# Talking-heads attention, Fourier mixing and an FFN: loads, statistics and the last transposes at the seam of two stages moved

## The chip, the cores and the metric

One core of a Trainium2 chip runs the kernel. The metric is device microseconds (us) of one execution, and less is better. Each engine has its own instruction stream and takes it in order: PE (TensorE, matmuls; its weight loads are shown as PEld), DVE (VectorE), ACT (ScalarE), POOL (GpSimd) and SP (SyncE, which here only issues DMAs). PE writes to PSUM; ACT and DVE evacuate from there to SBUF.

## What is computed

Two blocks follow each other, for 8 batches of 448 rows, 12 heads of 64, 768 columns, all in float32:

```python
scores = scale * q @ k^T                              # per batch and head
scores = einsum('bhij,hg->bgij', scores, w_pre)       # mix the heads
attn = exp(scores - max); attn = attn / (sum(attn) + 1e-9)
attn = einsum('bhij,hg->bgij', attn, w_post)          # mix them again
x = (attn @ v), heads side by side                    # 448 x 768 a batch
u = x + real(fft(fft(x, axis=1), axis=2))
un = (u - mean(u)) / sqrt(var(u) + 1e-6)
out = u + relu(un @ w_ch1) @ w_ch2                    # w_ch1 768 x 3072
```

## The kernel before

**Two stages.** `mix_phase` makes u of all batches and writes it to DRAM (`u_scr`, and `u_rev` for the mirrored rows). `ffn_phase` reads u back in 7 tiles of 512 rows and does the FFN. Both are matmul work on PE; a float32 matmul of the program is two records in the trace.

**Mixing.** A batch is 23 steps, all batches 184 steps, run by the loop at lines 932 to 964. In step s PE makes the pre-mix matmuls of step s+2 (L616, tile `mx`) and the post-mix matmuls of step s (L650, tile `po`), 16 records each. Between the two, DVE takes the maximum (L623), ACT the exponential (L630) and POOL the scaling by the row sum (L640). The mixing needs heads and rows side by side on partitions, so SP gathers each step's scores from tile `Sb` to tile `Kr` with four DMAs (L605), four steps ahead. The order of the operations within a step is written out by hand (`ORDERS`, two alternating lists).

**What fills the steps.** Other work is put between by due times. `due(kind, at, fn)` queues `fn` for step `at`; the kinds are `QK` (scores, L588, evacuated by ACT at L451), `AV` (attention times V, L680), `full` (transposes and Fourier matmuls) and `none` (loads and what needs no PSUM). `none` entries are issued at the start of a step (line 934). `full` and the PE kinds return evacuations that are queued in `pend` and issued at the next `flush`. Let f be the first step of the last batch (161): line 894 sets it. Around it:

- `emit_x` (L724): the transpose of the attention's result `XT` to `X`, four groups a batch, due at f+13, f+23, f+28 and f+29 (`AT_X`). A memset (L713) and a spill of the last AV group complete `XT` before the last two.
- `fold` (line 732, L745 to L766): sums and differences on POOL that the Fourier matmuls need, queued in `folds` and taken two a step until step f+19, later by `fold_rest`.
- `emit_z` (L789) and `emit_s2` (L805 on PE, L816 and L818 on DVE): the two Fourier stages. Those of a batch fall 39 to 49 steps after its start, so those of batch 6 run in the last batch's steps, and those of batch 7 in the FFN. After the last `emit_s2` of a pair, `store` writes u: plain DMAs on SP (L837), scattered ones on POOL (L828), and for the second pair a single row afterwards (L834), which two nested entries of the list `later` put two steps behind.
- V loads (L543) of the batch's own V at f+3 to f+7, on POOL; the loads of q and k for the next batch, which the last batch does not have; the conversion and storing of weights (`wts.deal`, L225 loads and L233 stores on POOL).

**The lead.** `_Lead` (line 319) prepares FFN tile 0 within the last mixing batch, so that the FFN can begin at once: `load` (L365) fetches its rows on POOL's queue, twelve DMAs, two a step; `stats` makes mean and variance on DVE (L370, L371); `power` makes the scale and shift on POOL (L375 to L378); `norm` applies them on ACT (L382); `turn` transposes on PE (L394) and evacuates half on ACT, half on DVE (L397); `total` makes differences of sub-blocks on DVE (L408). The rows' buffers are those of raw q and k, a ring of four.

**The FFN.** Both products use 7 products of sub-blocks in place of 8 (`ORDER`), with six chunks of the 3072 middle columns, two of them (`c` 0 and 1) of the kind the change touches. `first` multiplies a tile by a chunk of w_ch1: seven products of 12 records (L1169). `second` multiplies the result by w_ch2 (L1245), eight records for each product. In chunk 0 the same loop also prepares the next tile: its rows come in by `load_u` (L1064, SP), its statistics stand in `first` (L1085, L1086), its `power` after the last of them (L375 again), its `norm` (L1096) and `turn` (L1105, evacuated at L1107) in `second`. `store_ub` (L1119) writes a tile's sub-blocks to DRAM, for the next chunk.

**What sets the order.** Within `tc.manual_schedule(engines=...)` the named engines follow the program's order; the others are ordered by a planner with costs of its own. In mixing PE, DVE, ACT and POOL are named, in the FFN (chunks 0 and 1) PE and DVE. SP is never named, and DMAs that POOL issues can stand elsewhere than in the program's order too.

**The seam.** `mix_phase` returns after step f+29. What is left in `fill["full"]` (the z and s2 of batch 7) becomes `parts`, which `next_part` issues between FFN products: in tile 0's `second` after products 3 to 6, in tile 1's `first` after products 0 and 3 to 6. `ffn_phase` starts with line 1393:

```python
    with tc.manual_schedule(engines={ET.PE, ET.DVE, ET.Pool}):
        lead.total(3, pub)
        fold_rest()
```

Of the kernel before, what the change touches and what calls it, by code (L numbers as in the profile page):

```python
# [17 lines left out]
B, NH, S, D = 8, 12, 448, 64  # L18
# [394 lines left out]
def mix_phase(ctx, tc, rest, ident, q, k, v, w_pre, w_post, u_scr, u_rev, wts, lead):  # L413
# [6 lines left out]
    nc = tc.nc  # L420
# [27 lines left out]
    pend, folds, later = [], [], []  # L448
# [396 lines left out]
    def due(kind, at, fn):  # L845
        fill[kind].append((at, len(fill[kind]), fn))
# [4 lines left out]
    for b in range(B):  # L851
        f = b * GS
        at_t = [(a, nm, xx) for xx, at in enumerate(AT_T) for nm, a in zip("qk", at)]
        if b == 0:

            for i, xx in enumerate(START):
                for j, nm in enumerate("kq"):
                    for y in range(2):
                        due("none", -40, lambda xx=xx, nm=nm, y=y: emit_load_qk(0, xx, nm, y))
                    due("full", 2 * i + j - 20, lambda xx=xx, nm=nm: emit_xpose(0, xx, nm))  # L860
                for n in range(2):
                    due("QK", 2 * i + 2 + n - 20, lambda n=n, xx=xx: (emit_qk(n, xx), n))
            for pr in range(3):
                for y in range(2):
                    due("none", -40, lambda pr=pr, y=y: emit_load_v(0, pr, y))
        else:
            for at, (a, nm, xx) in zip(AT_L, sorted(at_t, key=lambda e: e[0])):
                for y in range(2):
                    due("none", f + at[y] - GS,
                        lambda b=b, xx=xx, nm=nm, y=y: emit_load_qk(b, xx, nm, y))  # L870
            for xx, at in enumerate(AT_T):
                for nm, a in zip("qk", at):
                    due("full", f + a - GS,
                        lambda b=b, xx=xx, nm=nm: emit_xpose(b, xx, nm))
        for pr in range(3 if b else 0):
            for y in range(2):
                due("none", f + AT_V[pr][y], lambda b=b, pr=pr, y=y: emit_load_v(b, pr, y))
        for n in range(0 if b else 2, NBL):
            for xx in range(3):
                due("QK", f + BLOCK_AT[n] - 7 + AT_QK[n][xx],  # L880
                    lambda n=NBL * b + n, xx=xx: (emit_qk(n, xx), n))
        for n in range(NG):
            for pr in range(3):
                due("AV", f + GROUP_AT[n + 1] + AT_AV[n][pr],
                    lambda a=b * NG + n, pr=pr: (emit_av(a, pr), None))
            at, gi = AT_X[n]
            due("full", f + at, lambda g=groups[b * NG + gi]: emit_x(g))
        for n, at in enumerate(AT_Z):
            due("full", f + at, lambda b=b, n=n: emit_z(b, n // 2, n % 2))
        for pair in range(2):  # L890
            for par in range(2):
                due("full", f + AT_S[pair][par],
                    lambda b=b, pair=pair, par=par: emit_s2(b, pair, par))
    f = (B - 1) * GS
    due("none", f, lambda: nc.gpsimd.memset(lead.mhalf[:, :], -0.5))
    for x in range(TB // P):
        for y in range(2):
            due("none", f + 1 + 2 * x + y, lambda x=x, y=y: lead.load(x, y))
        due("none", f + 8 + x, lambda x=x: lead.stats(x))
        due("none", f + (14, 15, 19, 20)[x], lambda x=x: lead.norm(x))  # L900
        due("full", f + 18 + 2 * x, lambda x=x: lead.turn(x, ms_tile))
    due("none", f + 12, lambda: lead.power(lead.mv))
    for n in range(3):
        due("none", f + 26 + n, lambda n=n: lead.total(n))
    due("none", 0, lambda: wts.deal(0))
    due("none", -39, emit_load_mix)
    due("none", -3, emit_mix)
# [23 lines left out]
    with tc.manual_schedule(engines={ET.PE, ET.DVE, ET.Activation, ET.Pool}):  # L931
        while s <= TOT - GS + AT_X[-1][0]:
            old = len(later)
            n = take("none", s)
# [35 lines left out]
            folds.pop(0)()  # L970

    def part(fn, tile_fn):
        while later:
            later.pop(0)()
        ms.append(tile_fn)
        if fn:
            for e in fn():
                e()
# [14 lines left out]
ORDER = (0, 4, 5, 1, 6, 2, 3)  # L993
# [11 lines left out]
def ffn_phase(ctx, tc, rest, ident, u_scr, u_rev, wts, ub_scr, out, fold_rest,  # L1005
# [4 lines left out]
    nc = tc.nc  # L1010
# [5 lines left out]
    pub = pool("pub", 3)  # L1016
# [29 lines left out]
    def next_part():  # L1046
        if parts:
            parts.pop(0)(lambda: ppx.tile([P, 512], F32, name="ms", tag="ms"))

    us, ubs, w1, w2, wt = {}, {}, {}, {}, {}  # L1050
# [59 lines left out]
    def total(t, n):  # L1110
        o, a, b = TOTALS[n]
        nc.vector.tensor_tensor(ubs[t, o][:, :, :], ubs[t, a][:, :, :],
                                ubs[t, b][:, :, :], op=ALU.subtract)
        if n == 3:
            store_ub(t)

    def store_ub(t):
        for i in ORDER:
            nc.sync.dma_start(out=ub_scr[t][i], in_=ubs[t, i][:, :, :])  # L1119

    H11, H22, H21, HS1, HS2, H12, H12S = range(7)
    LHS = (H11, H12, H12S, H22, HS1, HS2, H21)
# [21 lines left out]
    def first(n, st, beside):  # L1144

        c, t = divmod(n, NTB)
# [10 lines left out]
        for k, i in enumerate(ORDER):  # L1157
            if deep and t == 0:
                halves(ORDER2[k], (nc.vector, nc.gpsimd)[k % 2])
            if i in OPENS and ACC[i] not in ps:  # L1160
                ps[ACC[i]] = ps_tile(ACC[i])
            p = ps[ACC[i]].rearrange("p (m t) -> p m t", m=FM)
            ub = ubs.pop((n, i))
            for m in range(FM):
                for kc in range(NK):
                    for fn in beside.pop(done, ()):
                        fn()
                    done += 1
                    mm = nc.tensor.matmul(p[:, m, :], w1[i][:, kc, m * P:(m + 1) * P],  # L1169
                                          ub[:, kc, :],  # L1170
                                          start=i in (0, 4, 1)[:3 - seed] and m == kc == 0,
                                          stop=kc == NK - 1, skip_group_check=True)
                    if n == k == m == kc == 0:
                        tc.keep_in_program_order(mm)
            if i == 0 and seed:
                ps["Q"] = ps_tile("Q")
                nc.scalar.copy(out=ps["Q"][:, :], in_=ps["P"][:, :])
            elif i == 0:
                nc.scalar.copy(out=h11, in_=p)
            elif i == 4:  # L1180
                nc.scalar.copy(out=h22, in_=p)
            elif i == 5:
                nc.scalar.copy(out=h21, in_=p)
            elif i == 1 and seed:
                nc.scalar.activation(h11, p, ACTF.Relu)
            elif i == 1:
                vec.tensor_tensor(h11, h11, p, op=ALU.add)
                nc.scalar.activation(h11, h11, ACTF.Relu)
            elif i == 6:
                vec.tensor_tensor(h22, h22, p, op=ALU.add)  # L1190
                nc.scalar.activation(h22, h22, ACTF.Relu)  # L1191
                if deep:
                    quarters(nc.gpsimd, hq, h, H11, H22 + 1)
            elif i == 2:
                vec.tensor_tensor(h21, h21, p, op=ALU.add)
                nc.scalar.activation(h21, h21, ACTF.Relu)
            else:
                nc.scalar.activation(h12, p, ACTF.Relu)
            x = k - 3 * (n == 0)
            if norms and 0 <= x < NT2:  # L1200
                stats(t + 1, x)
                if x == NT2 - 1:
                    power(t + 1)
            if n == 1 and k not in (1, 2):
                next_part()
            if deep:
                wts.deal(DEALS[t > 0][k])
            elif i != 2:
                wts.deal(2 if norms else 3 if c == 0 else 4)
            if i == 2:  # L1210
                vec.tensor_tensor(hs1, h21, h22, op=ALU.add)
                vec.tensor_tensor(hs2, hs1, h11, op=ALU.subtract)
                if deep:
                    quarters(vec, hq, h, HS2, HS2 + 1)
                vec.tensor_tensor(h21, h11, h21, op=ALU.subtract)
            if t == NTB - 1 and c + 1 < NC:
                load_w1(c + 1, i)
            if NTB <= n + 1 < NC * NTB:
                new_ub(n + 1, i)
                nc.sync.dma_start(out=ubs[n + 1, i][:, :, :],  # L1220
                                  in_=ub_scr[(n + 1) % NTB][i])
# [168 lines left out]
    us[0] = lead.u  # L1390
    ET = mybir.EngineType
    with tc.manual_schedule(engines={ET.PE, ET.DVE, ET.Pool}):
        lead.total(3, pub)
        fold_rest()
    for i in ORDER:
        ubs[0, i] = lead.ub[i]
    with tc.manual_schedule(engines={ET.PE, ET.DVE}):
        for i in ORDER:
            load_w2(0, i)
        store_ub(0)  # L1400
        parts_ = [(c, k) for c in range(1, NC) for k in range(NK + FM)]
        for n in range(DEEP * NTB):
            c, t = divmod(n, NTB)
# [6 lines left out]
                load_u(n + 2)  # L1410
            st = {}
            first(n, st, {})
            second(n, st)
            if c == 0:
                wts.deal(1000)
# [98 lines left out]
```

## Time and profile before

| What | Value |
|---|---|
| median of 3 runs | 2360.4 us (2359.66 to 2360.79) |
| the profiled execution's own time | 2356.83 us |
| its span, first to last instruction | 2355.1 us |
| mean granted TensorE clock | 0.992 |
| steps of the last batch, f to f+22 | 718.2 to 810.6 us |
| last attention matmul (L680) starts | 823.15 us |
| first FFN product (L1169) starts | 830.72 us |
| mean rate of DMAs | 181 GB/s |

Times within the profile count from the span's start. A line such as `L650` is a line of the kernel. In a row of the timeline stand start, length, engine, line, operation, result tile <- input tiles, form and number of instructions; a bracket tells how long the engine stood idle before it and what ended that. In a row of waits stand the waiting engine, tile and line, what it waited for, the total, how often, and the longest. Busy shares are averages over stages with different limits; the two stages and their seam are therefore read apart.

### The profile page before, as it was taken

Reading aid. Unit: us, or ns where it says so; the run is one execution under the profiler, and the core shown is the slowest. Engines: PE = TensorE matmul, PEld = TensorE weight load, DVE = VectorE, ACT = ScalarE, POOL = GpSimd, SP = SyncE. Lnnn points to the kernel's source line nnn. Section 1 sums busy time; section 2 is a strip of 40 time slices with the busy share of each in tenths; the row PEclk is TensorE's granted clock in tenths of the full one; section 3 lists DMA queues with packets and bytes.
Section 4 is the critical chain, followed back from the end, with each engine's and each line's share of the span. In section 5 each row is a group of like instructions: output and inputs, shape, how many; then the busy total and the mean of one; then the engine's idle time right before and its main releaser. Section 6 shows DMA issues by size and latency. Waiting matters only on the chain.

```text
span 2355.1 us, 59472 instructions
## 1 busy us (share of the span) xinstructions
PE 2286.6 (97%) x22600; PEld 1717.5 (73%) x22600; DVE 1673.8 (71%) x3596; ACT 1103.0 (47%) x3085; POOL 1138.8 (48%) x1692
## 2 busy tenths in 40 slices
PE   6999999999999989999999999999999999999998
PEld 3455555554554667777777779998999999999998
DVE  3768777887777647785676766678776777776556
ACT  4766766676676522322222234443444344444434
POOL 3577977878777532121343443335333533443333
PEclk9999999999999999999999999999999999999999
DMA  7565655656646555567787876549546945684553
GB/s 161 160 174 175 178 177 155 199 171 181 188 150 189 193 180 195 178 223 269 225 208 230 241 240 181 144 138 271 149 132 169 258 125 166 175 229 107 148 129 67
DMA packets 213481, 425.60 MB, mean 181 GB/s; under 512 B 39080, under 2 KB 135744, under 8 KB 213198
## 3 DMA queue, kind: packets, MB, share of 16 engines
q1 hardware_dynamic: 141758, 278.78, 34.7%
q0 software_dynamic: 65440, 141.05, 27.4%
q8 instruction: 181, 2.97, 0.5%
q10 hardware_dynamic: 6000, 1.97, 0.4%
q14 instruction: 102, 0.84, 0.1%
HBM read 213.16 MB, written 129.39 MB: 145 GB/s over the span
## 4 chain that ended last, share of the span: by engine, by line
PE 57%; DVE 3%; issue 2%; DMA 1%; POOL 1%; ACT 0%; SPq 0%; POOLq 0%; DVEq 0%
PE psP L1169 17%; PE psP L1302 10%; PE psR L1169 9%; PE psR L1302 5%; PE psP L1245 5%; PE psQ L1169 4%; PE psR L1245 3%; PE psQ L1302 3%; PE psQ L1245 1%; PE psQ L1105 1%; DVE hq L1133 1%; DMA w<-wst 0%; DMA u<-u 0%; DMA w2t<-w 0%; POOL w L233 0%
## 5 line engine op out<-in xcount | busy, mean ns | idle before, releaser
L640 POOL TENSOR_SCALAR PP<-PP,rcp 128x448 f32<-128x448 f32 x368 | 234.8, 647 | 207.0 <-DVE rcp L638 165.0
L630 ACT ACTIVATE PP<-mx,nmx 128x448 f32<-128x448 f32 x368 | 230.2, 630 | 188.0 <-DVE nmx L623 174.3
L623 DVE TENSOR_REDUCE nmx<-mx 128x1 f32<-128x448 f32 x368 | 213.7, 618 | 137.3 <-PE mx L616 133.7
L1336 POOL DMA_DIRECT2D out_dram<-od x109 | 133.1, 1406 | 283.0 <-DVE od L1333 159.9
L1133 POOL TENSOR_TENSOR hq<-h 128x256 f32<-128x256 f32 (+1 forms) x168 | 104.3, 621 | 291.8 <-ACT h L1191 171.5
L616 PE MATMUL mx<-Kr,kw 60*32 60x448 f32 x2944 | 211.2, 551 | 15.6 <-DMA Kr<-Sb 14.1
L1333 DVE TENSOR_TENSOR od<-od 128x768 f32<-128x768 f32 x196 | 188.9, 975 | 52.5 <-ACT od L1330 50.6
L588 PE MATMUL ms<-kT,qT 64*32 64x448 f32 (+1 forms) x3072 | 205.0, 549 | 7.9 <-ACT qT L451 6.3
L663 DVE STREAM_TRANSPOSE Pv<-po 128x896 f32<-128x896 f32 x184 | 203.6, 1107 | 9.2 <-PE po L650 5.8
L451 ACT COPY Sb<-ms 124x448 f32<-124x448 f32 (+1 forms) x384 | 184.4, 540 | 42.1 <-PE ms L588 27.6
L650 PE MATMUL po<-PP,kw 60*32 60x448 f32 x2944 | 196.1, 543 | 2.0 <-issue 1.8
L1330 ACT COPY od<-psP 128x192 f32<-128x192 f32 x390 | 124.8, 320 | 146.6 <-PE psP L1302 142.2
L225 POOL DMA_DIRECT2D raw<-in_moe_w_ch_dram x88 | 52.8, 600 | 284.9 <-DVE tmp L269 269.4
L680 PEld LDWEIGHTS ms<-Pv,vv 64*64 64x64 f32 x5376 | 137.7, 132 | 70.6 <-issue 50.1
L1169 PE MATMUL psP<-qs,w1t 128*128 128x256 f32 x744 | 177.4, 379 | 0.0
L1169 PE MATMUL psP<-ks,w1t 128*128 128x256 f32 x744 | 176.9, 379 | 0.3 <-DVE h L1190 0.2
L680 PE MATMUL ms<-Pv,vv 64*64 64x120 f32 (+1 forms) x5376 | 160.2, 263 | 0.6 <-ACT X L451 0.3
L1245 PE MATMUL psP<-w2t,h 128*128 128x384 f32 x448 | 153.8, 486 | 0.5 <-DVE od L1265 0.5
L1169 PEld LDWEIGHTS psP<-ks,w1t 128*128 128x128 f32 x744 | 139.9, 190 | 19.0 <-DVE u L1252 0.7
L1169 PEld LDWEIGHTS psP<-qs,w1t 128*128 128x128 f32 x744 | 140.0, 190 | 17.4
L1190 DVE TENSOR_TENSOR h<-h,psP 128x512 f32<-128x512 f32 x42 | 28.8, 686 | 141.6 <-PE psP L1169 141.4
L1169 PE MATMUL psP<-ub,w1t 128*128 128x256 f32 x528 | 126.4, 379 | 0.0
(194 smaller groups left out, 5121.4 us busy)
## 6 DMA issues: line engine op xcount, KB each, us to landing
Kr<-Sb SPq DMA_DIRECT2D x736, 105.0 KB
out_dram<-od POOLq DMA_DIRECT2D x137, 384.0 KB
qs<-ub SPq DMA_DIRECT2D x89, 384.0 KB
ks<-ub SPq DMA_DIRECT2D x88, 384.0 KB
ub<-ub SPq DMA_DIRECT2D x79, 384.0 KB
w1t<-w SPq DMA_DIRECT2D x42, 384.0 KB
w2t<-w SPq DMA_DIRECT2D x42, 384.0 KB
raw<-in_moe_w_ch_dram POOLq DMA_DIRECT2D x56, 256.0 KB
```

The source lines that it names most:

```text
L588: nc.tensor.matmul(pss[x][o:o + hi - lo, :S], st["qT", xx][64 * x:64 * x + 64, y, lo:hi], st["kT", xx][64 * x:64 * x + 64, y, :], start=Tr ...
L616: nc.tensor.matmul(mx[x][64 * z + o:64 * z + o + 32, :S], kw1[64 * x:64 * x + KR, o:o + 32], Kr[64 * x:64 * x + KR, z, :], start=True, sto ...
L623: nc.vector.tensor_reduce(nmx[:, :], steps[T]["mx"][x][:, :S], axis=AX.X, op=ALU.max, negate=True)
L630: nc.scalar.activation(steps[T]["PP"][:, x, :], steps[T]["mx"][x][:, :S], ACTF.Exp, bias=steps[T]["nmx", x][:, :], accum_out=steps[T]["den ...
L640: nc.gpsimd.tensor_scalar(PP[:, x, :], PP[:, x, :], rcp[:, x:x + 1], 1.0, op0=ALU.mult, op1=ALU.mult)
L650: nc.tensor.matmul(po[o:o + 32, z, :S], kw2[64 * z:64 * z + KR, y, :], PP[64 * z:64 * z + KR, :, c * HS:(c + 1) * HS], start=True, stop=True)
L663: nc.vector.transpose(turned[a]["Pv"][:, j, :].rearrange("p (z s) -> p z s", z=2), steps[T]["po"][:, :, :S])
L680: nc.tensor.matmul(pss[y][64 * x:64 * x + 64, :nu * R], st["v", pr][64 * y:64 * y + 64, x, jb * D:(jb + 1) * D], _ap(Pv, 64 * y * rp + 32 ...
L1169: mm = nc.tensor.matmul(p[:, m, :], w1[i][:, kc, m * P:(m + 1) * P], ub[:, kc, :], start=i in (0, 4, 1)[:3 - seed] and m == kc == 0, stop= ...
L1245: nc.tensor.matmul(p, h[:, LHS[i], kf, x * P:(x + 1) * P], w2[i][:, kf, :], start=i in (0, 4, 1)[:3 - (c > 0)] and kf == 0, stop=kf == FM ...
L1302: nc.tensor.matmul(ps[j, key][:, :DQ], a, b, start=m in (0, 4), stop=True, skip_group_check=True)
L1333: eng.tensor_tensor(D[j][:, :, :], D[j][:, :, :], D[k][:, :, :], op=ALU.add)
```

## The change

It moves work, and adds or removes no computation. The last two X transposes of the last batch are due two steps later, which is after the loop's end, so that they become parts that tile 0's `first` issues after its first and second product; the folds that depend on them follow there. The lead's loads are due five steps sooner. Its statistics and norms become `full` entries, whose function is issued with the evacuations, and stand at other steps; `power` moves from f+12 to f+15. Two of its totals move behind the loop. In tile 0's `first` the statistics of tile 1 stand one product sooner. The store of tile 0's sub-blocks stands behind `first` in the program, and `part` empties the list `later` only as far as it reaches at its start, except in the last part.

```diff
@@ -884,6 +884,8 @@
             at, gi = AT_X[n]
+            if b == B - 1 and n > 1:
+                at += 2
             due("full", f + at, lambda g=groups[b * NG + gi]: emit_x(g))
...
@@ -892,16 +894,15 @@
     f = (B - 1) * GS
-    due("none", f, lambda: nc.gpsimd.memset(lead.mhalf[:, :], -0.5))
+    due("none", f + 1, lambda: nc.gpsimd.memset(lead.mhalf[:, :], -0.5))
     for x in range(TB // P):
         for y in range(2):
-            due("none", f + 1 + 2 * x + y, lambda x=x, y=y: lead.load(x, y))
-        due("none", f + 8 + x, lambda x=x: lead.stats(x))
-        due("none", f + (14, 15, 19, 20)[x], lambda x=x: lead.norm(x))
+            due("none", f - 4 + 2 * x + y, lambda x=x, y=y: lead.load(x, y))
+        due("full", f + (5, 9, 11, 13)[x], lambda x=x: [lambda: lead.stats(x)])
+        due("full", f + (15, 16, 19, 21)[x], lambda x=x: [lambda: lead.norm(x)])
         due("full", f + 18 + 2 * x, lambda x=x: lead.turn(x, ms_tile))
-    due("none", f + 12, lambda: lead.power(lead.mv))
-    for n in range(3):
-        due("none", f + 26 + n, lambda n=n: lead.total(n))
+    due("none", f + 15, lambda: lead.power(lead.mv))
+    due("none", f + 26, lambda: lead.total(0))
@@ -970,7 +971,9 @@
     def part(fn, tile_fn):
-        while later:
+        for _ in range(len(later)):
+            later.pop(0)()
+        while later and not fn:
             later.pop(0)()
@@ -1112,11 +1115,8 @@
         if n == 3:
-            store_ub(t)
-
-    def store_ub(t):
-        for i in ORDER:
-            nc.sync.dma_start(out=ub_scr[t][i], in_=ubs[t, i][:, :, :])
+            for i in ORDER:
+                nc.sync.dma_start(out=ub_scr[t][i], in_=ubs[t, i][:, :, :])
@@ -1196,13 +1196,15 @@
-            x = k - 3 * (n == 0)
+            x = k - 2 * (n == 0)
             if norms and 0 <= x < NT2:
                 stats(t + 1, x)
                 if x == NT2 - 1:
                     power(t + 1)
-            if n == 1 and k not in (1, 2):
+            if (n == 0 and k < 2) or (n == 1 and k not in (1, 2)):
                 next_part()
+                if n == 0 and k == 1:
+                    fold_rest()
@@ -1390,14 +1392,14 @@
     with tc.manual_schedule(engines={ET.PE, ET.DVE, ET.Pool}):
-        lead.total(3, pub)
+        for n in range(1, 4):
+            lead.total(n, pub)
         fold_rest()
...
-        store_ub(0)
...
             first(n, st, {})
+            if n == 0:
+                for i in ORDER:
+                    nc.sync.dma_start(out=ub_scr[0][i], in_=lead.ub[i])
             second(n, st)
```

## The prediction

> **What bounds the kernel now.** I read the page's busy table first, then PE's waits around the place of the change, then busy time in 4 us windows, last the order of time at the seam between the two stages. The page:
>
> ```profile
> PE 2286.6 (97%) x22600; PEld 1717.5 (73%) x22600; DVE 1673.8 (71%) x3596; ACT 1103.0 (47%) x3085; POOL 1138.8 (48%) x1692
> ```
>
> PE works 97% of the span and takes its work in written order, so a change that adds no matmul can only give or take PE's gaps. The gaps near the change, from PE's waits in 688 to 882 us (total, times, longest):
>
> ```profile
> PE psQ L1105 <- ACT un L1096: 4.3, 1, 4.3
> PE ms L724 <- DVE XT L713: 3.2, 1, 3.2
> PE mx L616 <- DMA Kr<-Sb: 3.1, 1, 3.1
> PE po L650 <- issue: 1.8, 1, 1.8
> ```
>
> The first two are the seam, the last two the middle of the last mixing batch. The second place is larger than its two rows. I took each step's length (start of its first post-mix matmul L650 to the next step's) less its matmuls at their undisturbed pace (start to start: 0.77 us for a group of pre-mix, 0.76 post-mix, 0.87 scores, 1.63 attention times V, 0.84 X). The step at 753.74 is 7.28 us long and holds 0.76 + 0.87 + 1.63 + 0.77 = 4.03: it loses 3.25; the one at 761.02 holds 2.40 in 5.76: 3.36. With f the first step of a batch, steps f+3 to f+10 lose 5.1, 3.2, 4.4, 3.4, 6.0 and 3.6 us in batches 1 to 6 (mean 4.3), but 11.9 in batch 7. What differs there are the DMAs that fetch the first FFN tile's rows (L365, twelve, about 0.53 us of POOL each, issued from 723 to 760). In 4 us windows (busy us with instructions in brackets for PE, PEld, DVE, ACT, POOL; then PE's clock, DMA share, GB/s), two before these loads, then four among and after them:
>
> ```profile
> 704.00:708.00 4.00, 4.00 (x84) 2.70 (x86) 2.61 (x7) 2.90 (x9) 1.25 (x2) 1.00 0.35 132
> 708.00:712.00 4.00, 4.00 (x96) 1.74 (x88) 2.90 (x7) 2.81 (x11) 1.41 (x2) 1.00 0.38 139
> ...
> 740.00:744.00 4.00, 4.00 (x64) 1.83 (x56) 2.50 (x5) 3.37 (x14) 3.90 (x7) 1.00 0.89 281
> ...
> 752.00:756.00 4.00, 2.69 (x56) 0.80 (x49) 2.36 (x6) 2.81 (x10) 3.49 (x6) 1.00 0.98 246
> ...
> 764.00:768.00 4.00, 2.22 (x32) 1.66 (x39) 1.90 (x5) 0.34 (x2) 3.49 (x6) 0.78 0.35 124
> ```
>
> DMA is near full (0.89, 0.98) and POOL too (3.90 of 4) where the loads and the V loads meet; then Kr comes late, PE stands, and its clock falls to 0.78. Five steps sooner DMA is at 0.35 and POOL at 1.25 to 1.41. The seam, in order of time (start, length):
>
> ```profile
> 825.12 1.50 DVE L408 TENSOR_TENSOR ks<-ks,qs 128x768 f32<-128x768 f32 x1
> 827.84 0.06 DVE L713 MEMSET XT<- 128x6 f32 x1
> 828.05 2.87 PE L724 MATMUL ms<-ident,XT 128*113 128x128 f32 x12 [3.17 <-DVE XT L713]
> ...
> 835.74 0.52 POOL L834 DMA_DIRECT2D v<-X  x1 [4.20 <-DMA v<-X,rows]
> ...
> 845.96 4.32 POOL L766 TENSOR_TENSOR xf<-xq 113x385 f32<-113x385 f32 x4
> ...
> 849.05 2.74 PE L1245 MATMUL psP<-w2t,h 128*128 128x384 f32 x8
> ...
> 852.39 0.21 DVE L1086 BATCH_NORM_AGGREGATE mv<-st 128x2 f32<-128x12 f32 x1
> 852.70 0.56 POOL L375 TENSOR_SCALAR mv<-mv 128x4 f32<-128x4 f32 x1 [2.42 <-DVE mv L1086]
> 856.12 1.54 PE L1105 MATMUL psQ<-ident,un 128*128 128x128 f32 x6 [4.32 <-ACT un L1096]
> 857.45 4.93 PE L1245 MATMUL psR<-w2t,h 128*128 128x384 f32 x8
> ```
>
> Two stalls. X's last transposes wait for a memset that stands behind the totals on DVE. Then FFN tile 1's first turn waits for its statistics, made last on DVE (852.6), then POOL's power (2.3 us) and ACT's norm (1.0). After it eight records take 4.93 instead of 2.74.
>
> **The change, part by part.**
>
> *Loads five steps sooner.* The same twelve DMAs, now at f-4 to f+3, about 704 to 735. Their buffers are free (the last transpose out of this ring is at f-6) and their source was written six batches ago, so they wait for nothing, and stand on POOL's queue where it idles 2.3 to 4.3 us a step: 6.2 us of issue at no cost, at f and later at the cost of a late scale L640, which has two steps of slack. What they leave behind is an ordinary batch's load. I put the loss at the mean of batches 1 to 6: 11.9 - 4.3 = 7.6 us gained, between 5.9 (batch 5's 6.0 stays) and 8.7 (batch 2's 3.2). If the loads are not the cause, 0.
>
> *Statistics and norms at the end of steps, power from f+12 to f+15.* Statistics are 1.23 us of DVE a tile and none of them is waited for in the trace. Norms are 1.05 to 1.14 us of ACT ahead of the exponentials; steps f+15 and f+16 lose 0.6 and 0.5 where other batches lose 0.3 and 0. Power's 2.0 us on POOL (779.53 to 781.53) now stand in a short step (2.81) ahead of L640: that may cost up to 1 us. The first norm now waits on ACT for power, one step after it is issued; behind it stand the next step's exponentials, and PE's matmuls behind these: within the same 1 us. Taken: 0.4 gained, between -1 and 0.8.
>
> *Seam, first half.* X's two transpose groups leave the end of mixing for behind the FFN's first and second product; three totals follow the memset. The last attention matmul ends at 823.15 + 1.73 = 824.9. The first product needs sub-blocks that were evacuated at 808.6 and weights issued from 802.8 to 808.2: it starts at 824.9. The memset comes at about 825.3, the first X group only at 827.5: no wait. Gained: 3.17, and the slow restart: twelve X records take 2.67 (830.72 - 828.05) instead of 2 x 0.84, 1.0 more, and the first product 2.79 instead of 2.59. Together 4.4. PE then ends the second stage's first product at 824.9 + 7 x 2.59 + 2 x 0.84 + 2.74 = 847.4 instead of 851.8.
>
> *Seam, second half.* Statistics come one product sooner: the last set follows the sixth product's add, at 824.9 + 6 x 2.59 + 1.7 + 0.7 + 1.2 = 844.1. Tile 1's rows no longer queue behind stores on SP that wait for totals, so they are issued from 824.9 instead of 828.4; they land before they are needed. Were POOL free, power would end at 846.4 and the norm at 847.4, no wait. But POOL is not free. Its folds of the second pair (L745 to L766) run from 836.27 to 850.28 and keep that place: they now wait for X groups copied at about 832.9, and for the row store L834, which waits until 835.7 for the scattered store ahead of it. In written order they come before power. So power ends at 850.3 + 2.3 = 852.6, the norm at 853.7: PE waits 6.3 us, and the turn starts 2.4 us sooner than at 856.1. If the scattered store lands sooner, folds start at 832.9 at best: 5.8. I take 3.0, near the row. The cold restart stays.
>
> [...] The rows show a slow restart after 3.06 and 3.17 us already (clock 0.78 in 764 to 768). [...]
>
> *Store of tile 0's sub-blocks, `part`'s loop, mhalf.* The stores are first read back seven tiles later; they move off SP's way to tile 1's rows, which is in the sum. The loop's new form delays only nested stores, and none is left at the first X part. The memset moves one step on an idle POOL. Tile 2's rows go where the last X groups' inputs lie, so their DMAs on SP now wait until about 832, still ahead of the 837.6 at which they are issued. Nothing, between -0.5 and 0.5.
>
> **Sum.** 7.6 + 0.4 + 3.0 = 11.0 us off the profiled execution's 2356.83: 2345.8. The runs' median is 3.6 above that execution, so 2349.4; I say 2349. Own range: gains of 5.9 - 1 + 2.4 = 7.3 to 8.7 + 0.8 + 5.8 = 15.3, that is 2345 to 2353.
>
> **Rivals.**
>
> *POOL is free for power.* If power gets ahead of the folds, the second half gives 8.7 and its cold restart goes (4.93 - 2.74 = 2.2): 10.9. With the rest 18.9: 2341.5. For it: the kernel leaves POOL's order in the FFN to a planner, and weight loads slip between the folds (838.17, 839.71). Against: folds are ready some 11 us before the statistics.
>
> *The loads are not the cause.* V loads, the scattered store and the weight stores meet in f+3 to f+9 in every batch, and batch 5 lost 4.7 in two steps with no such load. Then only 0.4 + 3.0 come: 2357.
>
> *Slower: the collision moves.* Batch 6's last outputs (718 to 720) and Kr gathers stand where the loads now go. If PE loses there what f+5 to f+10 lost (11.5) while the old place keeps a usual 4.3, f-4 to f+10 lose 15.8 instead of 12.2 now, and if POOL is later at the turn by its gain's 3 us, nothing pays it back: +3.6, 2364. It decides from a loss of 15.2 us there (12.2 and the seam's 3). Against it: DMA at 0.3 to 0.4 there, and a loss of about 0 now.
>
> **Chances.** Forecast 0.51, POOL free 0.16, loads not the cause 0.18, slower 0.15. A measurement of this kernel tells about 0.2% (4.7 us) from no change. Faster: 0.51 + 0.16 and a little of the third case, 0.70; same 0.15, slower 0.15. The range runs from 2340 to 2360: it takes in the POOL case and the case where the loads are not the cause, and leaves out the slower one and a gain beyond 20 us.
>
> **What will show it.** Right: no step of f+5 to f+10 losing over 2 us, L365 issued from about 704; the first FFN record directly after the last attention matmul, X groups behind the first two products; PE's wait before the first turn still there, at 4 to 6 us, with power's first instruction directly after L766. Wrong: Kr waits of 2 us and more in batch 7 as before or earlier; power before L766 (then the turn's wait is gone); an FFN product waiting for X, for weights or for rows of tile 1.

## The result and the profile after

The changed kernel takes 2353.57 us in the median of 22 runs, the kernel before 2359.67 in 22 runs beside them: ratio 0.9974, 95% interval 0.9967 to 0.9981. That is 6.1 us gained (4.5 to 7.8), where 11 were forecast. The profiled execution took 2355.12 us, its span 2353.3, its mean clock 0.992.

PE's busy time is the one line of the profile's page to set beside that of before (busy us, share of the span, instructions):

```profile
PE 2284.2 (97%) x22600; PEld 1715.1 (73%) x22600; DVE 1680.4 (71%) x3596; ACT 1102.9 (47%) x3085; POOL 1141.5 (49%) x1692
```

Nothing is to be read from it but that PE is still the engine that works through. PE's waits from 685 to 882 us of the changed kernel (total, times, longest) show what has changed:

```profile
PE psQ L1108 <- ACT un L1099: 7.2, 1, 7.2
PE po L650 <- issue: 1.4, 1, 1.4
...
PE mx L616 <- DMA Kr<-Sb: 0.6, 2, 0.3
```

Kr's wait fell from 3.1 to 0.6 us, X's wait for the memset (3.2) is gone, and the wait at the first turn of FFN tile 1 (the transposes of its normalized rows, `turn`) grew from 4.3 to 7.2. The last batch begins at f = 727.5, 9.3 us later than in the profile of before, and the loads L365 are issued from 712.5 to 744. In 4 us windows as in the prediction (the first among the loads, the other three where PE works least):

```profile
712.00:716.00 4.00, 4.00 (x72) 2.24 (x56) 2.61 (x7) 3.05 (x8) 2.80 (x5) 1.00 0.48 130
...
756.00:760.00 4.00, 3.44 (x56) 1.47 (x58) 1.81 (x3) 2.42 (x7) 3.94 (x8) 1.00 0.85 260
760.00:764.00 4.00, 3.40 (x84) 1.52 (x77) 1.91 (x5) 2.14 (x9) 3.00 (x5) 1.00 0.86 185
764.00:768.00 4.00, 3.23 (x76) 2.12 (x75) 1.32 (x3) 1.73 (x6) 1.42 (x3) 1.00 0.62 205
```

The first loads now meet a DMA share of 0.48. In the eight windows from 712 to 744 the share is 0.48 to 0.83, and PE is full (4.00) in all but the last (3.68). Later the share is at most 0.86 where it reached 0.98, PE works at least 3.23 of 4 where it fell to 2.69 and 2.22, and its clock stays at 1.00.

The seam of the changed kernel, in order of time (start, length; in brackets the idle time before and what ended it):

```profile
826.21 1.73 PE L680 MATMUL ms<-Pv,vv 64*64 64x120 f32 x56
827.87 2.86 PE L1169 MATMUL psP<-qs,w1t 128*128 128x256 f32 x12
830.57 0.82 PE L724 MATMUL ms<-ident,XT 128*113 128x128 f32 x6
...
838.22 0.53 POOL L834 DMA_DIRECT2D v<-X  x1 [3.63 <-DMA v<-X,rows]
...
839.86 1.98 POOL L745 TENSOR_TENSOR xs<-X 113x384 f32<-113x384 f32 x2
...
846.68 0.21 DVE L1089 BATCH_NORM_AGGREGATE mv<-st 128x2 f32<-128x12 f32 x1
847.42 2.74 PE L1247 MATMUL psP<-w2t,h 128*128 128x384 f32 x8
...
849.14 2.03 POOL L759 TENSOR_TENSOR xq<-xs 113x191 f32<-113x191 f32 x2
851.12 0.64 POOL L760 COPY xq<-xs 113x1 f32<-113x1 f32 x1
851.84 2.28 POOL L766 TENSOR_TENSOR xf<-xq 113x383 f32<-113x383 f32 x2
854.22 0.25 POOL L375 TENSOR_SCALAR mv<-mv 128x4 f32<-128x4 f32 x1
...
857.33 1.54 PE L1108 MATMUL psQ<-ident,un 128*128 128x128 f32 x6 [7.17 <-ACT un L1099]
858.66 3.48 PE L1247 MATMUL psR<-w2t,h 128*128 128x384 f32 x8
```

The first FFN product follows the last attention matmul (826.21 + 1.73 = 827.94) with no gap, and the X group stands behind it. The last statistics end at 846.9, but power (L375) starts only at 854.22, directly after the last fold (851.84 + 2.28 = 854.12): for 7.3 us the statistics wait on POOL's queue for folds that PE does not need yet. PE is done at 847.42 + 2.74 = 850.16 and waits until 857.33.

### The profile page after: what moved, and what is told of

It reads as the page before. It is cut to its first block, busy times and chain, and to the rows that moved or that the text cites. A ratio compares the mean times of both kernels' runs of the same rounds, so it can differ in the third digit from the quotient of the medians.

```text
span 2353.3 us, 59474 instructions
## 1 busy us (share of the span) xinstructions
PE 2284.2 (97%) x22600; PEld 1715.1 (73%) x22600; DVE 1680.4 (71%) x3596; ACT 1102.9 (47%) x3085; POOL 1141.5 (49%) x1692
## 4 chain that ended last, share of the span: by engine, by line
PE 84%; DMA 4%; DVE 4%; ACT 3%; POOL 2%; issue 2%; SPq 1%; ACTq 0%; DVEq 0%; POOLq 0%
PE psP L1169 18%; PE psP L1304 10%; PE psR L1169 9%; PE mx L616 6%; PE psP L1247 6%; PE psR L1304 5%; PE ms L680 5%; PE ms L588 5%; PE psQ L1169 5%; PE po L650 4%; DMA Kr<-Sb 3%; PE psR L1247 3%; PE psQ L1304 3%; PE ms L805 2%; PE psQ L1247 1%
## 5 line engine op out<-in xcount | busy, mean ns | idle before, releaser
L616 PE MATMUL mx<-Kr,kw 60*32 60x448 f32 x2944 | 216.5, 551 | 15.9 <-DMA Kr<-Sb 15.2
L650 PE MATMUL po<-PP,kw 60*32 60x448 f32 x2944 | 197.0, 541 | 1.4 <-issue 1.4
```

Source lines behind the costliest of these rows:

```text
L616: nc.tensor.matmul(mx[x][64 * z + o:64 * z + o + 32, :S], kw1[64 * x:64 * x + KR, o:o + 32], Kr[64 * x:64 * x + KR, z, :], start=True, sto ...
L650: nc.tensor.matmul(po[o:o + 32, z, :S], kw2[64 * z:64 * z + KR, y, :], PP[64 * z:64 * z + KR, :, c * HS:(c + 1) * HS], start=True, stop=True)
```

## The experiments

Two theories were set against each other for the seam: **POOL's order** (the held folds ahead of power set the turn) and **the statistics** (their end on DVE sets it, and power would not come sooner for being first). For the middle of the batch: **the loads** make the collision, or the V loads, stores and weights do it anyway. Each profile was cut into stages by the steps' first post-mix matmul L650. "Loss" is what steps f+3 to f+10 lost, as in the prediction; "end" is f+11 to f+22; "seam" runs from f+22 to tile 1's second turn; "behind" is the rest of the span; all in us:

```
profile               to f-4   loss   end   seam  wait at turn  behind
before                 702.0   11.8  38.2   51.6      4.3       1492.8
before, second copy    709.5   11.5  38.2   52.6      5.0       1491.7
before, third copy     710.7   12.7  38.2   50.4      4.3       1491.7
before, fourth copy    708.8    9.9  38.2   50.5      4.6       1491.5
statistics only        709.2    9.2  37.7   50.4      3.8       1492.1
loads only             705.5    3.8  38.4   49.8      4.1       1490.9
after                  711.3    6.1  37.7   48.3      7.2       1491.4
after, second copy     713.7    3.0  37.7   48.7      6.8       1491.4
after, third copy      708.5    3.2  37.7   49.7      6.9       1492.8
after, fourth copy     709.2    3.7  37.7   49.3      6.2       1491.9
seam only              711.2   11.6  38.2   48.9      7.3       1491.4
after, loads back      707.2    7.7  37.7   49.1      7.2       1495.4
seam only, power first 712.8   10.6  38.2   41.0      0         1492.1
after, power first     708.6    2.7  37.7   39.9      0         1492.1
```

Between f-4 and f+3, where the loads now stand, the loss is -0.1 us in every row: the collision did not move.

The ratios below have their 95% intervals in brackets. They are not the quotients of the medians beside them, which for the loads alone would be 0.9975 and for the seam alone 0.9971; the intervals hold these too.

**The loads alone.** The kernel before with the loads five steps sooner:

```diff
-            due("none", f + 1 + 2 * x + y, lambda x=x, y=y: lead.load(x, y))
+            due("none", f - 4 + 2 * x + y, lambda x=x, y=y: lead.load(x, y))
```

> The kernel before with one edit: the loads of the lead's rows five steps sooner. If these loads cause the loss in the last batch's steps f+3 to f+10 (11.9 us in the profile before, 6.1 after), this edit alone takes the loss to about 6 and the time to 5 to 6 us under the kernel before, 0.9975. If the loss is chance, or comes from the statistics and norms at the start of steps, the loss stays at 10 to 12 and the ratio is 1.000. If the collision only moves, steps f-4 to f+2 (loss 0.1 us in both profiles) lose what f+5 to f+10 gain, ratio 1.000.

Measured: 2357.07 us beside 2363.05, ratio 0.9981 (0.9967 to 0.9995). The loss falls from 11.4, the mean of the six rows with loads and statistics as before, to 3.8. PE's longest waits from 700 to 870 us in this kernel are those of the seam alone; no wait for Kr or vv is left:

```profile
PE psQ L1105 <- ACT un L1096: 4.1, 1, 4.1
PE ms L724 <- DVE XT L713: 3.1, 1, 3.1
...
```

It follows that the loads made most of the collision. Whether the DMAs themselves or POOL's queue is the tighter place there, no run separates.

**The seam alone.** The kernel before with the parts of the diff that touch the seam and the store, and the lead's dues as before. Its core:

```diff
+            if b == B - 1 and n > 1:
+                at += 2
...
-    for n in range(3):
-        due("none", f + 26 + n, lambda n=n: lead.total(n))
+    due("none", f + 26, lambda: lead.total(0))
...
-            x = k - 3 * (n == 0)
+            x = k - 2 * (n == 0)
```

> The kernel before with only the seam's part: X's last transposes behind the FFN's first two products, three totals behind the loop, the folds and stores where the change has them, tile 1's statistics one product sooner. The lead's loads, statistics, norms and power stay as before. My theory: the 3.2 us wait of X's transposes and its slow restart go (4.4 us), and PE's wait before tile 1's first turn grows from 4.3 to about 7 us because power stands behind the folds on POOL, so 1.5 to 3 us are left, ratio 0.999. A rival: the wait at the turn is set by the statistics on DVE or by tile 1's rows; then their sooner place keeps it at 4.3 us or less and the ratio is 0.998 or under.

Measured: 2356.24 us beside 2363.05, ratio 0.9981 (0.9967 to 0.9995). Its seam takes 48.9 us, as in the changed kernel, and its loss is 11.6, as before the change. PE's two longest waits from 700 to 880 us hold both:

```profile
PE psQ L1108 <- ACT un L1099: 7.3, 1, 7.3
PE mx L616 <- issue: 3.0, 1, 3.0
...
```

The two parts are thus separate: the wait of 7.3 belongs to the seam's order; the wait of 3.0 lies in the mixing, in step f+9, where the kernel before loses time too and none with early loads loses more than 1.1. The expectation had set a ratio of 0.999 for POOL's order and 0.998 or less for its rival; the time lies nearer to the rival's, with an interval that holds both, and it is the wait of 7.3 in place of 4.3 or less that speaks against the rival.

**The changed kernel with its loads back.**

```diff
-            due("none", f - 4 + 2 * x + y, lambda x=x, y=y: lead.load(x, y))
+            due("none", f + 1 + 2 * x + y, lambda x=x, y=y: lead.load(x, y))
```

> The changed kernel with the loads of the lead's rows back at f+1 to f+8; all else as changed. If the loads are the cause, the loss in f+3 to f+10 is again about 11 us and the time 5 to 6 us above the changed kernel, 0.9995 to 1.000 of the kernel before. If statistics and norms at the end of steps bring the gain, the loss stays at about 6 and the ratio at 0.9974. The difference to the run with the seam's part alone is what statistics, norms and power do by themselves: I expect 0.4 us or less.

Measured: 2358.33 us beside 2363.05, ratio 0.9987 (0.9973 to 1.0000). The collision returns, but with a loss of 7.7 and not 11.4. Two windows of this kernel:

```profile
760.00:764.00 4.00, 2.09 (x55) 1.68 (x51) 0.95 (x3) 0.97 (x2) 3.95 (x7) 0.93 0.95 182
764.00:768.00 4.00, 4.00 (x65) 1.41 (x57) 1.42 (x3) 1.25 (x7) 3.89 (x8) 0.65 0.71 219
```

DMA share 0.95 with POOL at 3.95, PE at 2.09 of 4, and the clock down to 0.65 in the next window: the picture of before. Only one step now loses much (f+8 3.7; f+9 and f+10 0.4 each), where before f+9 and f+10 lost 3.4 and 1.6 besides.

**The statistics alone.** By the diffs, that difference can only come from the new places of statistics, norms and power or from chance, so they were tried by themselves:

```diff
...
-        due("none", f + 8 + x, lambda x=x: lead.stats(x))
-        due("none", f + (14, 15, 19, 20)[x], lambda x=x: lead.norm(x))
+        due("full", f + (5, 9, 11, 13)[x], lambda x=x: [lambda: lead.stats(x)])
+        due("full", f + (15, 16, 19, 21)[x], lambda x=x: [lambda: lead.norm(x)])
...
-    due("none", f + 12, lambda: lead.power(lead.mv))
+    due("none", f + 15, lambda: lead.power(lead.mv))
```

> The kernel before with only the lead's statistics, norms and power at their new places; loads and seam as before. Taken in the prediction at 0.4 us gained, all of it in f+11 to f+22: then the loss in f+3 to f+10 stays at 11 to 12 us and the ratio is 0.9998 to 1.000. If statistics at the start of steps hold up DVE while they wait for late rows, the loss there falls to about 8 us as in the run with the loads put back, ratio 0.9985.

Measured: 2362.98 us beside 2363.86, ratio 0.9988 (0.9971 to 1.0004), not to be told from no change by time. The stages tell more: loss 9.2, and f+9 and f+10 lose 0.4 each, as with the loads back. PE's two longest waits from 700 to 882 us:

```profile
PE psQ L1105 <- ACT un L1096: 3.8, 1, 3.8
PE ms L680 <- DMA vv<-in_v_dram: 3.5, 1, 3.5
...
```

PE still waits for vv, once, and the steps behind lose little. So in these two profiles the new places of statistics, norms and power save 2.9 us of the loss (11.4 less 8.45, the mean of 9.2 and 7.7) as long as the loads come late, and about nothing once they come soon (3.8 with the old places, 2.7 to 6.1 with the new). Before, sets of statistics (1.23 us each) ran on DVE at 752.0, 758.8 and 763.8, in and between the two worst steps; that this is the reason was not tried set by set.

**Power ahead of the held folds.** The changed kernel, with four folds issued where all of them were and the rest only behind power, by a written order on POOL. Its core:

```diff
-    def fold_rest():
-        while folds:
+    def fold_rest(n=99):
+        while folds and n > 0:
             folds.pop(0)()
+            n -= 1
...
                 if x == NT2 - 1:
-                    power(t + 1)
+                    last = power(t + 1)
+                    if n == 0:
+                        with tc.issue_after(last.ins):
+                            fold_rest()
...
                 if n == 0 and k == 1:
-                    fold_rest()
+                    fold_rest(4)
```

> The changed kernel with one edit on POOL in the FFN's first tile: the folds of the second pair's second half and the four sums after them are held behind tile 1's power instead of ahead of it. All the work is done. If POOL's queue sets the turn's wait, power starts when the statistics are there, some 7 us sooner, the 7.2 us wait of PE at the first turn falls under 1 us and its slow restart goes: 7 to 8 us under the changed kernel, ratio to the kernel before 0.994. If rows or statistics set it, the wait stays at 4 us or more. A cost that could take it back: the first Fourier matmuls of the last batch need the held folds, and would wait for them by up to 3 us.

Measured: **2346.64 us** beside 2363.05, ratio 0.9933 (0.9914 to 0.9952): it beats both kernels. Its seam, in order of time:

```profile
840.84 0.21 DVE L1090 BATCH_NORM_AGGREGATE mv<-st 128x2 f32<-128x12 f32 x1
841.14 0.26 POOL L375 TENSOR_SCALAR mv<-mv 128x4 f32<-128x4 f32 x1 [4.15 <-DVE mv L1090]
841.58 2.74 PE L1251 MATMUL psP<-w2t,h 128*128 128x384 f32 x8
...
843.12 2.78 POOL L745 TENSOR_TENSOR xs<-X 113x384 f32<-113x384 f32 x2
844.26 0.87 PE L1109 MATMUL psQ<-ident,un 128*128 128x128 f32 x6
844.97 2.75 PE L1251 MATMUL psR<-w2t,h 128*128 128x384 f32 x8
...
850.99 1.95 POOL L766 TENSOR_TENSOR xf<-xq 113x383 f32<-113x383 f32 x2
...
856.00 0.94 PE L789 MATMUL ms<-ts,xf 113*97 113x113 f32 x8
```

POOL now stands idle for 4.15 us and takes power as soon as DVE has made the last statistics. The turn at 844.26 has no wait, the product behind it runs at full pace (2.75 us), and the folds end at 852.94, before PE asks for them at 856.00. The wait that the expectation allowed for there did not come. The statistics theory is out: in the changed kernel they had been ready 7.3 us before power began, and power does come sooner for being first. Now it is the statistics that POOL waits for, but PE no longer waits for either.

**The seam alone, power first.** The same edit on the kernel that has only the seam's part:

```diff
...
                 if x == NT2 - 1:
-                    power(t + 1)
+                    last = power(t + 1)
+                    if n == 0:
+                        with tc.issue_after(last.ins):
+                            fold_rest()
...
                 if n == 0 and k == 1:
-                    fold_rest()
+                    fold_rest(4)
```

> The kernel before with the seam's part and with tile 1's power ahead of the held folds; the lead's loads, statistics, norms and power in mixing as before. If POOL's queue at the turn is what took the seam's gain back, this is worth the seam alone plus the turn's wait and its slow restart: the time from the last step's post-mix to the second turn falls from 51.6 to about 40 us, and the ratio to the kernel before is 0.9950 to 0.9955. If the large gain of power first came from anything in the last batch's steps, it is 0.998 as with the seam alone.

Measured: 2353.69 us beside 2363.86, ratio 0.9953 (0.9941 to 0.9965). Seam 41.0 us, no wait at the turn; loss 10.6, as in the other kernels with late loads. The two gains stay separate here too.

**Copies.** Both kernels unchanged, three times more each, since their stages gave a larger gain than their times:

> The kernel before, a second profile of it, for the spread of one kernel's stages between executions. The first profile reached f-4 at 702.0 us and the five others, whose instructions are the same up to there, at 705.5 to 711.3. If that is spread alone, this one lies anywhere in 702 to 712; if the kernel before is steadily sooner, at 702 again. The loss in f+3 to f+10 should be 8 to 12 us, the turn's wait 4.1 to 4.3 us.

> The changed kernel, a second profile. The loss in f+3 to f+10 should be 2 to 6 us, the turn's wait about 7.2 us, as the order on POOL is fixed; f-4 anywhere in 702 to 712 us.

> The kernel before, once more. In dispute is the time up to four steps ahead of the last mixing batch's boundary, a stretch in which both kernels give every engine the same instructions in the same order: 702.0 to 709.5 us in the four profiles so far without the seam part (mean 706.5), 707.2 to 713.7 in the six with it (mean 710.8). Chance: anywhere from 702 to 714, and the two means move towards each other. A steady cost of the changed program: 703 to 709 here.

> The changed kernel, once more, for the same stretch. Chance: anywhere from 702 to 714. Steady: 709 to 714. The stages behind it as before: loss around the boundary 3 to 6, seam 48 to 49 us.

> The kernel before, a third copy, for the same stretch as the first: chance 702 to 714, steady 703 to 709.

> The changed kernel, a third copy, for the same stretch as the second: chance 702 to 714, steady 709 to 714.

Measured (one execution each): 2363.85, 2364.05 and 2359.25 us for the kernel before; 2354.86, 2352.22 and 2352.24 for the changed one. The loss and the seam repeat within about 3 us (the table's rows); the turn's wait varies more than was expected, 4.3 to 5.0 us before and 6.2 to 7.2 after. The stretch up to f-4, where nothing differs, took 702.0 to 710.7 us before (mean 707.8) and 708.5 to 713.7 after (mean 710.7). In the last two pairs the means are 709.8 and 708.8, where in the first two they were 705.8 and 712.5. A steady cost of the changed program would have put the last two of before at 703 to 709 and the last two of the changed kernel at 709 to 714; they came at 710.7 and 708.8, and at 708.5 and 709.2.

## Why the prediction was right, and where not

- **The time lies in the stated range, and that alone shows little.** 2353.57 us lies within 2340 to 2360, but so do the sums of two rivals (2341.5 and 2357), and it lies 0.6 above the sum's own range of 2345 to 2353. The gain of 6.1 lies between the forecast's 11.0 and the 3.4 of the rival in which the loads do nothing, and nearer to the latter. What tells the cases apart are the stages and the waits.
- **Loads, 7.6 us forecast: right.** Loss 11.4 in the six rows with loads and statistics as before, 3.7 in the five with the change's (6.1, 3.0, 3.2, 3.7, 2.7): 7.6. "No step of f+5 to f+10 losing over 2 us" was just missed in the first profile (f+6 2.1, f+8 2.3) and held in the copies (most 1.3). That they are not the cause is refuted by the loads alone (3.8) and by the loads put back. But the parts do not simply add: the early loads alone give all of it, while taking them back out of the changed kernel costs only 4.0 (3.7 to 7.7), because some 2.9 of the 11.4 can be had by the statistics' places too. The prediction had priced these at nothing in this stretch, because no row waited for them.
- **How idle the loads' new place was: misread, at no cost.** The prediction put DMA there at 0.35 and POOL at 1.25 to 1.41, from the first two windows of eight. Two further windows of the kernel before, whose own loads begin at 723:

```profile
716.00:720.00 4.00, 4.00 (x95) 1.71 (x86) 3.84 (x10) 3.73 (x14) 1.81 (x3) 1.00 0.58 197
720.00:724.00 4.00, 4.00 (x58) 2.69 (x62) 3.96 (x10) 2.29 (x6) 3.68 (x7) 1.00 0.69 213
```

DMA is at 0.58 and 0.69 there, and POOL at 3.68 in the second. The loads cost nothing there all the same (-0.1 from f-4 to f+3).
- **End of steps, 0.4: right.** 38.2 to 37.7, and 37.7 with the statistics alone.
- **Seam, first half: right in kind and size.** No wait before the first product, X behind it, and PE done with the second stage's first product 850.16 - 827.94 = 22.2 us after the last attention matmul, forecast 847.4 - 824.9 = 22.5.
- **Seam, second half: right in kind, the wait 0.9 us too small.** The folds kept their place and power came directly after L766. The turn's wait was put at 6.3 us in the sum, and at 4 to 6 among the signs of being right, and came to 7.2 (6.2 to 6.9 in the copies), because POOL was done 854.12 - 827.94 = 26.2 us after the last attention matmul instead of 25.4: L834's wait (to 838.22, 10.3 us behind that matmul against 10.9 before) gave 0.6 back, and the last folds took longer, L759 2.03 us instead of 1.14 and L760 0.64 instead of 0.18. The whole seam gained 1.9 us (50.9, the mean of six, to 49.0, the mean of six), under the 2.4 of the forecast's own row and the 3.0 taken.
- **The rival "POOL is free for power"** is not what this change does, but its price for the seam was right: 10.9 forecast, 50.9 to 40.5 = 10.4 measured with power first. The slower rival needed 15.2 us of loss up to f+10; at most 6.0 came.
- **Where the sum failed: 11.0 forecast, 6.1 timed.** Two terms of it. The seam's 3.0 came to 1.9, so the stages of the change give 7.6 + 0.5 + 1.9 = 10.0. And the sum takes the stages' gain for the whole kernel's. The four profiled executions of each kernel differ by 7.4 us as a whole (mean times 2361.0 and 2353.6), which agrees with the timed 4.5 to 7.8; but their stages from f-4 on differ by 10.3, and the stretch up to f-4 took 2.9 of it back.
- **Whether that stretch is chance stays open.** Over all profiles it took back 2.7 (707.6 in the six without the seam's order, 710.3 in the eight with it), although every engine has the same instructions there in the same order. With a spread of about 3 us between executions of either group, that is 1.7 times its standard error. For chance speak the last two pairs of copies, which point the other way; and the stretch behind the seam varies as well, by 4.5 us (1490.9 to 1495.4). Against chance alone: the profiles come from several chips, and compared within one, the kernels with the seam's order are 3.5 us later on the first (three profiles against one), 3.9 later on the second (two against two), and 1.0 sooner on the third (two against two).
- **Stages and times of the other kernels** agree only within wide bounds. The loads alone gain 8.5 us by their stages and 4.5 by their ratio, power first 20.2 and 15.8; but the seam alone 1.8 and 4.5, seam with power first 10.6 and 11.1, statistics alone 3.1 and 2.8, and loads back 5.9 and 3.1, with intervals of 3 to 4.5 us to either side. The profiled execution need not be a typical one: that of the loads alone (2348.78) was the second fastest of 12 (2348.67 to 2362.79), that of power first (2341.43) the second fastest of 6, that of the seam alone (2361.63) 5.4 above its median. Whether the early loads give some 4 us less in executions other than the profiled ones stays open: a time without a profile has no stages.

## What to carry to other kernels

When work becomes ready sooner, read what stands ahead of the next short instruction on its engine's queue: here 14 us of folds (839.86 to 854.12) that nobody was waiting for yet stood ahead of 2 us that PE was waiting for, and holding some of the folds back by hand gained 8.5 us in the seam (49.0 to 40.5), where the whole change had gained 6.1. The same twelve loads cost nothing here where DMA stood at 0.48 to 0.83 with PE at 4.00 of 4 in seven windows of eight, while at their old place, with DMA at up to 0.98 and POOL at 3.49 to 3.90, the loss was 7.6 us larger (11.4 against 3.8 with the loads alone moved); the stretch that lost time told where not to put them. A gain added up from one profile's stages should be set against the spread of the stages that nobody touched, here 9 us in one kernel.

## What the runs showed of the hardware

**Behind PE's long waits at the seam the clock stood at 0.50 for 3.4, 6.8 or 10.2 us, and the length of the wait did not tell which.** The prediction had taken 4.93 us for the eight records behind the turn, and 2.2 us of loss, as the price of a wait of 4.32. In windows of the changed kernel cut at the clock's steps:

```profile
850.00:853.20 3.20, 0.17 (x1) 0.00 (x0) 3.20 (x5) 0.00 (x0) 3.12 (x5) 1.00 0.02 7
...
856.80:859.80 3.00, 2.47 (x8) 2.01 (x9) 0.00 (x0) 2.77 (x5) 0.00 (x0) 0.50 0.00 0
860.20:863.60 3.40, 3.40 (x15) 2.17 (x15) 1.11 (x2) 1.15 (x4) 0.00 (x0) 1.00 0.02 5
```

The clock is at 0.50 from 853.3 to 860.1, 6.8 us; PE works in the last 2.8 of them, and the eight records take 3.48 us although the wait was 7.17. In the third copy of the same kernel the clock is low from 847.1 to 857.4, 10.2 us, and after a wait of 6.90 the eight records take 5.02:

```profile
847.20:857.30 10.10, 5.85 (x14) 3.73 (x15) 0.72 (x2) 3.83 (x5) 2.80 (x6) 0.50 0.01 2
...
857.40:860.00 2.60, 2.60 (x14) 1.75 (x13) 0.76 (x2) 1.77 (x3) 0.00 (x0) 1.00 0.00 0
```

Other copies had 3.4 us (second copy of before, 865.2 to 868.6, 3.55 us for the records). So in the copies of the changed kernel, with waits of 6.2 to 7.2 us, these eight records lost 0.7 to 2.3 us from execution to execution, and a single profile gives one draw of it. In these four profiles the loss grows with what is left of the low stretch when the turn starts: with 2.8 us left the records take 3.48, with 3.7 left 3.94 (fourth copy of after), with 5.7 left 4.93 (before), with 5.9 left 5.02.

In the first profile of the kernel before, the three low stretches from 700 to 882 us begin at 766.27, 827.71 and 855.01 and last 3.4, 3.4 and 6.8 us. They go with the waits of 3.06 us (for Kr, ended at 765.78), 3.17 (for X's memset) and 4.32 (at the turn):

```profile
766.30:769.60 3.30, 3.30 (x48) 1.79 (x30) 1.85 (x3) 1.34 (x4) 1.19 (x2) 0.50 0.38 138
827.75:831.10 3.35, 3.05 (x13) 3.04 (x14) 1.39 (x3) 1.57 (x4) 3.19 (x5) 0.50 0.92 307
855.05:861.80 6.75, 5.68 (x13) 3.69 (x14) 0.55 (x1) 3.81 (x5) 0.00 (x0) 0.50 0.01 2
```

Nor was PE always idle up to the fall. The first of these falls came 0.5 us after the wait's end, and with the statistics alone the turn started at 860.19, after its wait of 3.8 us, and the clock fell at 861.12, when PE had worked again for 0.9 us:

```profile
857.71:861.10 3.39, 0.91 (x7) 0.91 (x8) 0.44 (x1) 1.99 (x3) 1.20 (x3) 1.00 0.00 0
...
861.20:864.50 3.30, 3.30 (x6) 1.69 (x5) 0.56 (x1) 1.52 (x3) 0.00 (x0) 0.50 0.02 5
```

What makes a low stretch 3.4, 6.8 or 10.2 us long, no run here separates.
